# Doubled transfers and an fe row layout by transposing DMA in a joint-network training step

## The chip, the core and the metric

The kernel runs on one core of a Trainium2 chip. The metric is the device time of one execution in microseconds (us). The times below are of several executions; one more execution was recorded by the hardware profiler, and every profile line here comes from such a recording.

## The reference, cut to what matters

The reference computes a small speech model forward and then all gradients. Two convolutions of three taps with stride 2 and a tanh-approximated gelu turn `x` (2 x 16000 x 256) into `f` (2 x 4000 x 256). The joint network adds a projection of `f` to one of `g` (8 rows a batch), takes a tanh and projects again.

```python
h = gelu(conv3(x, w1))[:, ::2, :]
f = gelu(conv3(h, w2))[:, ::2, :]
fe = einsum("btd,de->bte", f, w_f)
ge = einsum("bud,de->bue", g, w_g)
j  = tanh(fe[:, :, None, :] + ge[:, None, :, :])
out = einsum("btud,dv->btuv", j, w_o)
# and the gradients of x, w1, w2, g, w_f, w_g, w_o for a given grad_out (2, 4000, 8, 256)
```

All inputs and outputs are bf16.

## The kernel before

The 4000 rows of `f` in each batch are cut into chunks: 256, seven of 512 and 160 rows in the first batch, seven of 512, then 256 and 160 in the second, 18 in all. A chunk whose rows are a multiple of 128 is called whole; the two of 160 rows aren't. In a whole chunk partition p holds nb adjacent rows (nb = 2 or 4), so that block a of 128 columns holds rows nb*p + a.

The main loop (L1170) runs over steps. Step k holds three stages of three different chunks side by side:

- `stage_j` of chunk k, the joint network. It runs over four pairs of `u` (`pair`, L759). For a pair, ACT makes `JT` = tanh(fe + ge) in column layout (channels on partitions, L766), while DVE adds (`JR`, L779) and ACT takes the tanh (L786) of the same values in row layout (rows on partitions), from `FER`, the row-layout fe. PE makes the output from `JT` and `WO`, the gradient of `w_o` from `JR` and the rows of grad_out (`GO_R`), and the gradient of `j` from the transposed grad_out (`GOT`). DVE multiplies the latter by 1 - j^2 (`JSQ`, `NGZ`) and sums over `u` in `ZS`. The output leaves through `OUT_SB`.
- `stage_a` of chunk k+1: the odd and even columns of the first convolution (`HTo`, `HTe`), the second convolution (`FT`), and `FE`, each with the gelu's derivative (`G1o`, `G1e`, `G2`). `shift` (L357) makes the column shifted by one row across blocks in a tile of its own: `HS` of `HTo`, `G1S` of `G1o`. `to_rows` (L642) turns `FE` into `FER` by TensorE transposes and one copy from PSUM.
- `stage_de` of chunk k-1: the backward pass through both convolutions and all weight gradients but that of `w_o`. The row layouts it needs (`HRo`, `HRs`, `HRe`, `FR`, `NFR`, `GFR`, `GHoR`, `GHeR`) are made by transposing DMAs within SBUF (`dma_rows`, L621). The gradient of `x` leaves through `GX_SB`, one block of 128 rows at a time.

All loads and all transposing DMAs are issued by SP, one instruction stream in order; all stores of outputs by POOL. Matmuls stand in one helper line, L412. `psb` is a PSUM tile of bf16, `ps` one of fp32.

The order of instructions on each engine is fixed by a planner in the kernel itself (`Flow`, L44 to L263). Every operation has a cost estimate, a due time and the buffers it needs. The planner simulates the engines, orders the operations by due time, then goes back from the end three times to set new due times, and keeps the best order. A DMA is taken to be done its queue's work plus 2.0 us plus a margin after its issue; the margin is 6.5 us (`MARGIN`, L49) unless the operation says otherwise. Each class of buffers is a ring with a fixed number of slots (L336); an operation that opens a new buffer waits in the plan until a slot is free.

Of the kernel before, what the change touches and what calls it, by code (L numbers as in the profile page):

```python
# [10 lines left out]
BF16 = mybir.dt.bfloat16  # L11
FP32 = mybir.dt.float32
ALU = mybir.AluOpType
# [265 lines left out]
def kernel(  # L279
# [56 lines left out]
    for name, n in (("xc", 1), ("xh", 2), ("xs", 1), ("hto", 2), ("hs", 2), ("ft", 2), ("g1e", 3), ("g1o", 3), ("g1s", 3), ("g2", 3),  # L336
                    ("fe", 2), ("fer", 2), ("gsq", 2), ("gs", 2), ("jt", 3), ("got", 3), ("go", 7), ("out", 6), ("rows", 4),
                    ("hte", 2), ("jr", 3), ("hro", 2), ("hrs", 2), ("hre", 2), ("fr", 2), ("jsq", 2), ("ngz", 2), ("ghe", 1), ("gho", 1),
                    ("ghs", 1), ("gf", 1), ("gfs", 1), ("gfh", 2), ("ngfe", 1), ("x5", 2), ("gx", 3), ("ghh", 2)):
        F.cls(name, n)  # L340
# [145 lines left out]
    def load_got(g_, up, h, at):  # L486
        S = st[g_]
        if h == 0:
            S.setdefault("GOT", {})[up] = buf("got", [P, NB, 2, KT, P], BF16, "GOT")
        GOT, GO = S["GOT"][up], S["GO"][up, h]  # L490
        dma("SP", lambda: GOT[:, 2 * h:2 * h + 2].rearrange("p a u k q -> p (a u k) q"),
            lambda: GO[:].rearrange("p a u v -> p (a u v)"), r=[GO], w=[(GOT, h)], bytes_=2 * P * 1024,
            new=[GOT] if h == 0 else [], transpose=True, at=at, margin=2000.0 if g_ == 0 else None)

    def load_gor(g_, up, h, at, hold=()):
        b, ci, c0, W = chunks[g_]
        GO = buf("go", [P, 2, 2, V], BF16, "GO_R")
        lo, hi = 2 * h * P, min(W, (2 * h + 2) * P)
        nb, rem = (hi - lo) // P, (hi - lo) % P
        src = grad_out[b, c0 + lo:c0 + hi, 2 * up:2 * up + 2, :].rearrange("t u v -> t (u v)")  # L500
        if whole[g_]:
            rows_ = grad_out[b, c0:c0 + W, 2 * up:2 * up + 2, :].rearrange("(p a) u v -> p a (u v)", p=P)
            dma(LOADQ, lambda: GO[:].rearrange("p a u v -> p a (u v)"), lambda: rows_[:, 2 * h:2 * h + 2], r=[], w=[(GO, "m")],
                bytes_=2 * P * 1024, new=[GO], at=at, hold=hold, margin=2000.0 if g_ == 0 else None)
            nb = rem = 0
# [8 lines left out]
        st[g_].setdefault("GO", {})[up, h] = GO  # L514
# [65 lines left out]

    def conv_gelu(W, taps, h_buf, h_ap, g_buf, g_ap, news):

        sq = buf("gsq", [P, KT, CW], BF16, "g_sq")
        s = buf("gs", [P, KT, CW], BF16, "g_s")
        for mt in range(KT):
            ps = psum()

            def mms(e, mt=mt, ps=ps):
# [9 lines left out]
                out=h_ap(mt), in_=ps[:, :W], func=ACT.Gelu_apprx_tanh), r=[ps], w=[(h_buf, mt)])  # L598
# [12 lines left out]
            out=sq[:, :, :W], in0=sq[:, :, :W], in1=h_ap(None), op=ALU.mult), r=[sq, (h_buf, 0), (h_buf, 1)], w=[sq], at=late)  # L611
# [51 lines left out]
    def stage_a(g_, t0, dt):  # L663
# [3 lines left out]
        HTo = colbuf("hto", g_, "HTo")  # L667
        G1o = colbuf("g1o", g_, "G1o")
        HTe = colbuf("hte", g_, "HTe")
        G1e = colbuf("g1e", g_, "G1e")  # L670
        S["HTo"], S["G1o"], S["G1e"] = HTo, G1o, G1e
        both = lambda T_: (lambda mt: T_[:, mt, 0:W] if mt is not None else T_[:, :, 0:W])
# [3 lines left out]
        conv_gelu(W, (taps, S["XCk"] + [W1]), HTo, both(HTo), G1o, lambda: G1o[:, :, 0:W], [HTo, G1o])  # L676
        shifted = []
        for cls, nm, T_ in (("hs", "HTo", HTo), ("g1s", "G1o", G1o)):
            if ci == 0:
                h, hr = None, []  # L680
            else:
                pv, pw = st[g_ - 1][nm], chunks[g_ - 1][3]
                h, hr = (lambda pv=pv, pw=pw: pv[:, :, pw - 1:pw]), [(pv, 0), (pv, 1)]
            shifted.append(shift(cls, g_, cls.upper(), lambda lo, hi, T_=T_: T_[:, :, lo:hi], [(T_, 0), (T_, 1)], h, hr))
        HS, S["G1S"] = shifted
# [4 lines left out]
        conv_gelu(W, (taps, S["XCk"] + [W1, S["XS"]]), HTe, both(HTe), G1e, lambda: G1e[:, :, 0:W], [HTe, G1e])  # L690
        pad_tail(g_, HTo)
        pad_tail(g_, HTe)
# [4 lines left out]
        taps = [(lambda i=i, kt=kt: W2[:, i, kt], 0, lambda SRC=SRC, kt=kt: SRC[:, kt, 0:W])  # L697
                for i, SRC in ((2, HTo), (1, HTe)) for kt in range(KT)]
        taps += [(lambda kt=kt: W2[:, 0, kt], lo, lambda f=f, kt=kt: f(kt)) for lo, f in back(g_, HS, HTo, W) for kt in range(KT)]
        S["go"] = [conv_gelu(W, (taps, [(HTo, 0), (HTo, 1), HS, (HTe, 0), (HTe, 1), W2]), FT, both(FT), G2,  # L700
                             lambda: G2[:, :, 0:W], [FT, G2])]
# [3 lines left out]
        S["FE"] = FE  # L705
        for mt in range(KT):
            ps = psum()

            def mms(e, mt=mt, ps=ps):
                for kt in range(KT):  # L710
                    mm(ps[:, :W], WF[:, kt, mt * P:(mt + 1) * P], FT[:, kt, :W], kt == 0, kt == KT - 1)
            pe_first(mt == 0, "fe", c_pe([W] * KT), mms, r=[(FT, 0), (FT, 1), WF], w=[ps], new=[ps] + ([FE] if mt == 0 else []))
            evac(lambda mt=mt: FE[:, mt, :W], lambda ps=ps: ps[:, :W], W, r=[ps], w=[(FE, mt)])
        pad_tail(g_, FE)
        S["FER"] = to_rows("fer", FE, 0, nb_of[g_] * P, [0, 1, "z"])
        F.now = t0 + A_AT[3] * dt
        late = [start_of[g_] + HR_AT[2] * W] * 2 if g_ < 2 else [t0 + HR_AT[0] * dt, t0 + HR_AT[1] * dt]
        HRo = col_rows("HRo", "hro", g_, HTo, ["z"], late[0])
        R0 = dma_rows("HRs", "hrs", g_, lambda: HS[:].rearrange("p k w -> p (k w)"), [HS], 1, late[0])
        if wh:  # L720
            S["HRs"] = [R0, HRo], lambda m, bl, d2: HRo.cols(m, bl - 1, d2) if bl else R0.cols(m, 0, d2)
        else:
            R1 = buf("hrs", [P, KT * P], BF16, "HRs")
            for kt in range(KT):
                dma("SP", lambda kt=kt: R1[:, kt * P:(kt + 1) * P], lambda kt=kt: HTo[:, kt, P - 1:2 * P - 1],
                    r=[(HTo, kt), (HTo, "z")], w=[(R1, kt)], bytes_=P * P * 2, new=[R1] if kt == 0 else [], transpose=True, nb=late[0])
            S["HRs"] = [R0, R1], lambda m, bl, d2: R1[:m, d2 * P:(d2 + 1) * P] if bl else R0.cols(m, 0, d2)
        HRe = col_rows("HRe", "hre", g_, HTe, ["z"], late[1])
        FR = col_rows("FR", "fr", g_, FT, ["z"], late[0])
        for nm, R in (("HRo", HRo), ("HRe", HRe), ("FR", FR)):  # L730
            S[nm] = [R], R.cols
# [24 lines left out]
    def stage_j(g_, t0, dt):  # L756
        b, ci, c0, W = chunks[g_]
        S = st[g_]
        def pair(up):  # L759
# [4 lines left out]
            for j in range(2):  # L764
                for mt in range(KT):
                    op("ACT", c_act(W, ptr=True), lambda e, j=j, mt=mt: nc.scalar.activation(  # L766
                        out=JT[:, j, mt, :W], in_=S["FE"][:, mt, :W], func=ACT.Tanh,
# [6 lines left out]
            for h, tbs in enumerate(halves):  # L774
# [15 lines left out]
                GO = S["GO"].pop((up, h))  # L790

                def gwo(e, tbs=tbs, JR=JR, GO=GO):
                    for tb, m in tbs:
                        for j in range(2):
                            for d2 in range(KT):
                                n = gwo_cnt[0]
                                mm(GWO[:, d2, :], JR[:m, tb % 2, j, d2 * P:(d2 + 1) * P], GO[:m, tb % 2, j, :],
# [3 lines left out]
            OUTS = [buf("out", [P, 2, 2, V], BF16, "OUT_SB") for _ in halves]  # L801
            for step in range(4):
# [41 lines left out]
                for tb, m in nblk[g_]:  # L844
# [3 lines left out]
                    OUT = OUTS[tb // 2]  # L848

                    def out_mm(e, tb=tb, m=m, ps=ps):  # L850
                        for jj in range(2):
# [3 lines left out]
                    pe_first(tb % 2 == 0, "out", c_pe([V] * 4), out_mm, r=[JT, WO], w=[ps], new=[ps] + ([OUT] if tb % 2 == 0 else []))  # L855
                    evac(lambda tb=tb, m=m, OUT=OUT: OUT[:m, tb % 2].rearrange("p u v -> p (u v)"), lambda m=m, ps=ps: ps[:m, :], 512,
                         r=[ps], w=[(OUT, tb % 2)])
            for h, OUT in enumerate(OUTS):
                F.now = tu + q * (h + 1) / 2
                lo, hi = 2 * h * P, min(W, (2 * h + 2) * P)  # L860
                nb, rem = (hi - lo) // P, (hi - lo) % P
                dst_ = out_0[b, c0 + lo:c0 + hi, 2 * up:2 * up + 2, :].rearrange("t u v -> t (u v)")
                if whole[g_]:
                    rows_ = out_0[b, c0:c0 + W, 2 * up:2 * up + 2, :].rearrange("(p a) u v -> p a (u v)", p=P)
                    dma(STOREQ, lambda rows_=rows_, h=h: rows_[:, 2 * h:2 * h + 2],
                        lambda OUT=OUT: OUT[:].rearrange("p a u v -> p a (u v)"), r=[OUT], w=[], bytes_=2 * P * 1024)
                    continue
                if nb:
                    dma(STOREQ, lambda dst_=dst_, nb=nb: dst_[0:nb * P].rearrange("(a p) n -> p a n", p=P),
                        lambda OUT=OUT, nb=nb: OUT[:, 0:nb].rearrange("p a u v -> p a (u v)"),  # L870
                        r=[(OUT, t_) for t_ in range(nb)], w=[], bytes_=nb * P * 1024)
                if rem:
                    dma(STOREQ, lambda dst_=dst_, nb=nb: dst_[nb * P:],
                        lambda OUT=OUT, nb=nb, rem=rem: OUT[:rem, nb].rearrange("p u v -> p (u v)"),
                        r=[(OUT, nb)], w=[], bytes_=rem * 1024)
# [351 lines left out]
```

## Time and profile before

| | us |
|---|---|
| median of 8 runs | 802.78 |
| lowest and highest run | 801.51, 805.07 |
| profiled execution, device time | 801.51 |
| its span, first to last instruction | 799.7 |
| mean granted TensorE clock | 0.997 of full speed |

The profiled execution is the lowest of the eight runs. PE is TensorE's matmuls, PEld its weight loads, DVE the vector engine, ACT the scalar engine, POOL GpSimd, SP the engine that issues DMAs. Busy shares are of the span; a pipelined matmul is recorded for longer than the time until the next one ends, so PE's share isn't its share of peak. The DMA share is the mean over 16 DMA engines of the time that packets took; packets overlap, so it can exceed 1. A waiting time is idle time of an engine just before an instruction, with what ended it.

The DMA queue of SP moved 133.25 MB, that of POOL 49.19 MB; all together 184.74 MB, 231 GB/s on average.

### The profile page before, as it was taken

How to read it: one execution, taken by the hardware profiler on the slowest of the kernel's cores; microseconds unless marked ns; L12 is line 12 of the kernel's file. 1: busy time of each engine (PE TensorE's matmuls, PEld its weight loads, DVE VectorE, ACT ScalarE, POOL GpSimd, SP SyncE). 2: the span in 40 equal slices, each digit the busy share in tenths (PEclk: the TensorE clock that was granted, in tenths of full speed). 3: DMA queues.
4: the chain of work that ended last, by engine and by line, in shares of the span. 5: the costliest groups of instructions: out<-in, count | busy, mean ns of one | idle time of the engine just before them, and what ended most of it. 6: DMA issues, size and time to landing. Idle time of an engine off the chain costs nothing.

```text
span 799.7 us, 17623 instructions
## 1 busy us (share of the span) xinstructions
PE 776.3 (97%) x6196; PEld 576.7 (72%) x6196; DVE 753.8 (94%) x1756; ACT 715.0 (89%) x1164; POOL 221.5 (28%) x461
## 2 busy tenths in 40 slices
PE   8788999999999999999999999999999999999997
PEld 6555667686776867787776668676776767778885
DVE  5999999998989999997989999999999999999995
ACT  5999999999999999997899999989898999898572
POOL 1212232321222222343232142222223132233242
PEclk9999999999999999999999999999999999999999
DMA  8999999999999999999999999999999899999974
GB/s 202 229 207 217 212 248 259 248 224 259 201 266 216 257 259 233 238 247 255 222 224 228 220 211 244 225 254 259 254 239 263 199 216 259 250 236 235 206 203 114
DMA packets 384700, 184.74 MB, mean 231 GB/s; under 512 B 331716, under 2 KB 368358, under 8 KB 384612
## 3 DMA queue, kind: packets, MB, share of 16 engines
q1 hardware_dynamic: 366644, 133.25, 86.8%
q0 software_dynamic: 15584, 49.19, 19.2%
q10 hardware_dynamic: 2384, 1.18, 0.6%
q8 instruction: 48, 0.79, 0.5%
q14 instruction: 40, 0.33, 0.1%
HBM read 52.48 MB, written 50.34 MB: 129 GB/s over the span
## 4 chain that ended last, share of the span: by engine, by line
PE 72%; DVE 11%; ACT 3%; DMA 1%; issue 1%; DVEq 0%; ACTq 0%
PE ps L412 61%; PE GWO L412 10%; DVE NGZ L833 2%; DVE ZS L841 2%; DMA GFR<-GF 1%; DVE JR L779 1%; DVE g_s L599 1%; DVE GHo L954 1%; DVE ACC L894 1%; PE psb L652 1%; DVE GHe L964 1%; ACT JR L786 1%; DVE g_sq L610 0%; DVE G1o L617 0%; DVE g_sq L607 0%
## 5 line engine op out<-in xcount | busy, mean ns | idle before, releaser
L766 ACT ACTIVATE JT<-FE,GE 128x512 bf16<-128x512 bf16 (+2 forms) x288 | 181.9, 676 | 5.7 <-PE ps L412 5.7
L440 POOL DMA_DIRECT2D out_dram<-OUT_SB x136 | 95.0, 700 | 243.4 <-ACT OUT_SB L423 151.7
L412 PE MATMUL ps<-GOT,WT 128*128 128x512 bf16 (+3 forms) x640 | 151.8, 334 | 2.7 <-DMA GOT<-GO_R 2.0
L412 PE MATMUL ps<-WO,JT 128*128 128x256 bf16 x1024 | 151.8, 273 | 2.3 <-DVE NGZ L833 0.8
L833 DVE SCALAR_TENSOR_TENSOR NGZ<-JSQ,ps 128x512 f32<-128x512 bf16 (+2 forms) x252 | 151.0, 605 | 2.0 <-PE ps L412 1.8
L786 ACT ACTIVATE JR<-JR 128x1024 bf16<-128x1024 bf16 x128 | 136.3, 1069 | 6.2 <-DVE JR L779 6.1
L412 PE MATMUL GWO<-GO_R,JR 128*128 128x256 bf16 x1024 | 132.4, 273 | 2.3 <-ACT JR L786 2.3
L823 ACT ACTIVATE JSQ<-JT 128x1024 bf16<-128x1024 bf16 (+2 forms) x132 | 126.5, 959 | 8.8 <-DVE NGZ L833 6.9
L412 PEld LDWEIGHTS <-JT 128*128 128x128 bf16 x1024 | 98.6, 98 | 47.3 <-issue 5.7
L841 DVE TENSOR_TENSOR ZS<-ZS,NGZ 128x512 f32<-128x512 f32 (+2 forms) x216 | 130.9, 613 | 0.1
L423 ACT CAST OUT_SB<-ps 128x512 bf16<-128x512 f32 x208 | 119.0, 597 | 8.5 <-PE ps L412 8.3
L412 PEld LDWEIGHTS <-JR 128*128 128x128 bf16 x1028 | 99.7, 98 | 25.4 <-ACT JR L786 3.4
L412 PEld LDWEIGHTS <-WT 128*128 128x128 bf16 x1000 | 88.4, 98 | 39.0 <-issue 3.8
L412 PEld LDWEIGHTS <-W 128*128 128x128 bf16 x792 | 69.6, 98 | 55.2 <-issue 2.9
L412 PE MATMUL ps<-XC,W 128*128 128x512 bf16 (+4 forms) x432 | 92.6, 342 | 2.2 <-DMA XC<-in_x_dram 1.2
L779 DVE TENSOR_TENSOR JR<-FER,GEB 128x1024 bf16<-128x1024 bf16 x128 | 87.3, 684 | 0.1
L412 PEld LDWEIGHTS <-X 128*128 128x128 bf16 x768 | 74.9, 98 | 10.7 <-issue 0.2
L440 POOL DMA_DIRECT2D out_dram<-GX_SB x70 | 38.9, 557 | 145.7 <-ACT GX_SB L425 113.5
L599 DVE SCALAR_TENSOR_TENSOR g_s<-g_sq,ps 128x512 bf16<-128x512 bf16 (+2 forms) x108 | 65.7, 609 | 9.9 <-ACT HTo L597 8.2
L412 PE MATMUL ps<-WT,GHo 128*128 128x256 bf16 x384 | 73.0, 273 | 0.2
L894 DVE TENSOR_TENSOR ACC<-ACC,ps 128x512 f32<-128x512 f32 x96 | 64.2, 676 | 9.3 <-PE ps L412 9.1
L595 ACT ACTIVATE g_sq<-ps 128x512 bf16<-128x512 f32 (+2 forms) x108 | 58.4, 546 | 9.3 <-PE ps L412 8.9
(137 smaller groups left out, 1280.8 us busy)
## 6 DMA issues: line engine op xcount, KB each, us to landing
GO_R<-in_grad_out_dram SPq DMA_DIRECT2D x120, 256.0 KB, 4.2
out_dram<-OUT_SB POOLq DMA_DIRECT2D x120, 256.0 KB, 4.7
X<-in_x_dram SPq DMA_DIRECT2D x28, 576.0 KB, 6.3
out_dram<-GX_SB POOLq DMA_DIRECT2D x60, 256.0 KB, 4.5
GOT<-GO_R SPq DMA_TRANSPOSE x128, 5.3
out_dram<-w_out SPq DMA_DIRECT2D x9, 128.0 KB, 2.0
GO_R<-in_grad_out_dram SPq DMA_DIRECT2D x8, 128.0 KB, 3.7
out_dram<-OUT_SB POOLq DMA_DIRECT2D x8, 128.0 KB, 3.2
```

Of the source, the lines that this page charges most:

```text
L412: nc.tensor.matmul(ps_ap, lhsT=lhsT, rhs=rhs, start=start, stop=stop)
L423: nc.scalar.copy(out=dst(), in_=src())
L440: return eng_.dma_start(out=out(), in_=in_())
L595: op("ACT", c_act(W, True), lambda e, mt=mt, ps=ps: nc.scalar.activation(out=sq[:, mt, :W], in_=ps[:, :W], func=ACT.Square, scale=GELU_SQR ...
L599: op("DVE", c_dve(W), lambda e, mt=mt, ps=ps: nc.vector.scalar_tensor_tensor(out=s[:, mt, :W], in0=sq[:, mt, :W], scalar=1.0, in1=ps[:, :W ...
L766: op("ACT", c_act(W, ptr=True), lambda e, j=j, mt=mt: nc.scalar.activation(out=JT[:, j, mt, :W], in_=S["FE"][:, mt, :W], func=ACT.Tanh, bi ...
L779: op("DVE", c_dve(n * 2 * D, 0.5), lambda e, lo=lo, n=n, m=m, JR=JR: nc.vector.tensor_tensor(out=JR[:m, lo % 2:lo % 2 + n], in0=S["FER"][: ...
L786: op("ACT", c_act(n * 2 * D), lambda e, lo=lo, n=n, m=m, JR=JR: nc.scalar.activation(out=JR[:m, lo % 2:lo % 2 + n], in_=JR[:m, lo % 2:lo % ...
L823: nc.scalar.activation(out=JSQ[:, :, :W], in_=JT[:, j, :, :W], func=ACT.Square)
L833: op("DVE", c_dve(W) + 6, lambda e, d2=d2, ps=ps, u=u, zap=zap, JSQ=JSQ: nc.vector.scalar_tensor_tensor(out=zap(), in0=JSQ[:, d2, :W], sca ...
L841: op("DVE", c_dve(W), lambda e, d2=d2, dst=dst, NGZ=NGZ: nc.vector.tensor_tensor(out=dst[:, d2, :W], in0=ZS[:, d2, :W], in1=NGZ[:, :W], op ...
L894: op("DVE", c_dve(512), lambda e: nc.vector.tensor_tensor(out=acc_ap().rearrange("p k d -> p (k d)"), in0=acc_ap().rearrange("p k d -> p ( ...
```

## The change

In words:

- `GO_R`, `GOT` and `OUT_SB` hold all blocks of a chunk for a pair of `u` and are moved by one DMA instead of one for each half. Rings: `go` 7 halves to 4 wholes, `out` 6 halves to 3 wholes.
- In whole chunks, two blocks of `GX_SB` share one tile and leave with one DMA, with 4 KB instead of 2 KB in a row. Ring `gx` 3 single to 2 double.
- In whole chunks `FE` lies block-major (block, then half of the channels), written and read through strided patterns, and `FER` is made by one transposing DMA on SP. The 160-row chunks keep the TensorE transposes.
- `HTo` and `HTe` lie in one tile `HT`, the shifted block in front of `HTo`; one DMA makes `HR` out of all three. `G1o` has its shifted block in front too. The second convolution then reads each tap of `HTo` in one run, and `GHo` takes one DVE instruction instead of two. Rings: `hto`, `hte`, `hs` of 2 become `hh` of 2; `hro`, `hrs`, `hre`, `fr` of 2 become `hr`, `hrs`, `fr` of 1.
- `GHo` and `GHe` lie in one tile `GH`, and one DMA makes `GHR`. Ring `rows` 4 to 2, `ghr` 1.

```diff
-    ... ("hto", 2), ("hs", 2), ("ft", 2), ("g1e", 3), ("g1o", 3), ("g1s", 3), ("g2", 3),
-        ("fe", 2), ("fer", 2), ("gsq", 2), ("gs", 2), ("jt", 3), ("got", 3), ("go", 7), ("out", 6), ("rows", 4),
-        ("hte", 2), ("jr", 3), ("hro", 2), ("hrs", 2), ("hre", 2), ("fr", 2), ("jsq", 2), ("ngz", 2), ("ghe", 1), ("gho", 1),
-        ("ghs", 1), ("gf", 1), ("gfs", 1), ("gfh", 2), ("ngfe", 1), ("x5", 2), ("gx", 3), ("ghh", 2)):
+    ... ("hh", 2), ("ft", 2), ("g1e", 3), ("g1o", 3), ("g2", 3),
+        ("fe", 2), ("fer", 2), ("gsq", 2), ("gs", 2), ("jt", 3), ("got", 3), ("go", 4), ("out", 3), ("rows", 2), ("ghr", 1),
+        ("jr", 3), ("hr", 1), ("hrs", 1), ("fr", 1), ("jsq", 2), ("ngz", 2), ("gh", 1),
+        ("ghs", 1), ("gf", 1), ("gfs", 1), ("gfh", 2), ("ngfe", 1), ("x5", 2), ("gx", 2), ("ghh", 2)):
...
+    def load_got(g_, up, at):
+        S, n = st[g_], nb_of[g_]
+        GOT, GO = buf("got", [P, NB, 2, KT, P], BF16, "GOT"), S["GO"][up]
+        S.setdefault("GOT", {})[up] = GOT
+        dma("SP", lambda: GOT[:, 0:n].rearrange("p a u k q -> p (a u k) q"),
+            lambda: GO[:, 0:n].rearrange("p a u v -> p (a u v)"), r=[GO], w=[GOT], bytes_=n * P * 1024,
+            new=[GOT], transpose=True, at=at, margin=2000.0 if g_ == 0 else None)
...
+    def part(B_, view):
+        p_ = Buf(None, None, None, B_.name)
+        p_.view = lambda _: view(B_.t)
+        return p_
...
+        HT = buf("hh", [P, KT * (2 * CW + P)], BF16, "HT")
+        HTo = part(HT, lambda t_: t_[:, 0:ns].rearrange("p (k w) -> p k w", k=KT))
+        HTe = part(HT, lambda t_: t_[:, ns:ns + nc_].rearrange("p (k w) -> p k w", k=KT))
...
-                for i, SRC in ((2, HTo), (1, HTe)) for kt in range(KT)]
-        taps += [(lambda kt=kt: W2[:, 0, kt], lo, lambda f=f, kt=kt: f(kt)) for lo, f in back(g_, HS, HTo, W) for kt in range(KT)]
+                for i, SRC, lo in ((2, HTo, P), (1, HTe, 0), (0, HTo, r0)) for kt in range(KT)]
...
+        if wh:
+            FE.view = lambda t_: t_[:, 0:KT * n * P].rearrange("p (b k q) -> p k b q", k=KT, q=P)
...
-        S["FER"] = to_rows("fer", FE, 0, nb_of[g_] * P, [0, 1, "z"])
+        if wh:
+            FR_ = S["FER"] = buf("fer", [P, NB, D], BF16, "FER")
+            dma("SP", lambda: FR_[:, 0:n].rearrange("p b (k q) -> p (b k) q", q=P), lambda: FE.t[:, 0:KT * n * P],
+                r=[(FE, 0), (FE, 1)], w=[FR_], bytes_=KT * n * P * P * 2, new=[FR_], transpose=True)
+        else:
+            pad_tail(g_, FE)
+            S["FER"] = to_rows("fer", FE, 0, n * P, [0, 1, "z"])
...
-        HRo = col_rows("HRo", "hro", g_, HTo, ["z"], late[0])
-        R0 = dma_rows("HRs", "hrs", g_, lambda: HS[:].rearrange("p k w -> p (k w)"), [HS], 1, late[0])
...
-        HRe = col_rows("HRe", "hre", g_, HTe, ["z"], late[1])
-        FR = col_rows("FR", "fr", g_, FT, ["z"], late[0])
+        HR = buf("hr", [P, KT * (2 * CW + P)], BF16, "HR")
+        dma("SP", lambda: HR.t[:, 0:ns + nc_].rearrange("p (g q) -> p g q", q=P), lambda: HT.t[:, 0:ns + nc_], r=[HT], w=[HR],
+            bytes_=(ns + nc_) * P * 2, new=[HR], transpose=True, nb=late[0])
...
+        FR = col_rows("FR", "fr", g_, FT, ["z"], late[1])
...
-            OUTS = [buf("out", [P, 2, 2, V], BF16, "OUT_SB") for _ in halves]
+            OUT = buf("out", [P, NB, 2, V], BF16, "OUT_SB")
...
+        GHR = buf("ghr", [P, 2 * KT * CW], BF16, "GHR")
+        dma("SP", lambda: GHR.t[:, 0:2 * nc_].rearrange("p (g q) -> p g q", q=P), lambda: GH.t[:, 0:2 * nc_], r=ghk, w=[GHR],
+            bytes_=2 * nc_ * P * 2, new=[GHR], transpose=True)
...
+                    dma(STOREQ, lambda s0=s0 - 1, sn=sn, lo=lo, hi=hi, dst=dst: bass.AP(
+                        tensor=dst.tensor, offset=dst.offset + (4 * (s0 + sn * lo) - 3) * D, ap=[[4 * sn * D, hi - lo], [1, 8 * D]]),
+                        lambda GX2=GX2, lo=lo, hi=hi: GX2[:].rearrange("p a c d -> p (a c d)")[lo:hi], r=[GX2], w=[],
+                        bytes_=(hi - lo) * 4096, cost=550.0)
```

`GO_R`'s load, which now fetches a whole pair, has the same form as the new `load_got`. `late` holds the earliest due times of the row layouts: 0.7 (`late[0]`) and 0.4 (`late[1]`) of the step before the chunk's own.

## The prediction

> **What bounds the kernel now.** I read the page's busy shares first, then the busy time by stages, then the chain of waits inside one step, then the groups by form, the waits and the DMA issues.
>
> ```profile
> PE 776.3 (97%) x6196; PEld 576.7 (72%) x6196; DVE 753.8 (94%) x1756; ACT 715.0 (89%) x1164; POOL 221.5 (28%) x461
> ```
>
> Three engines are near full, so the page's shares don't say which one sets the end. Time by stages (columns: stretch, length, then busy us and instruction count of PE, PEld, DVE, ACT, POOL, then PE clock, DMA share, GB/s):
>
> ```profile
> 0.00:80.00 80.00, 67.20 (x515) 47.34 (x516) 69.22 (x183) 69.99 (x123) 16.67 (x44) 0.98 1.01 214
> 80.00:360.00 280.00, 278.25 (x2154) 203.87 (x2154) 271.56 (x594) 266.37 (x417) 76.94 (x154) 1.00 1.12 240
> 360.00:480.00 120.00, 117.82 (x951) 85.89 (x950) 112.26 (x269) 108.20 (x180) 36.39 (x76) 1.00 1.10 227
> 480.00:760.00 280.00, 278.66 (x2225) 210.64 (x2223) 270.34 (x613) 249.71 (x402) 76.04 (x154) 1.00 1.10 238
> 760.00:800.00 40.00, 34.35 (x359) 28.98 (x357) 30.40 (x101) 20.68 (x45) 15.48 (x35) 0.98 0.62 158
> ```
>
> From 80 to 760 us PE idles 5.3 of 680 us. PE's idle time lies at the ends: 12.8 us in the first 80 (there DVE and ACT are the full ones) and 5.7 in the last 40. Is a busy PE really at its rate? The chain, one whole 512-row step (start us, us, what):
>
> ```profile
> 234.34 4.76 PE ps L412 x26
> ...
> 259.55 0.87 PE GWO L412 x8
> 260.42 0.45 PE psb L652 x8
> 260.87 2.39 PE ps L412 x18
> ...
> 281.79 4.76 PE ps L412 x26
> ```
>
> Every piece between is PE; the same work starts again after 47.45 us. Eight 256-column matmuls take 0.87 us (109 ns each), two 512-column ones 0.43 (217 ns each), so 0.417 ns a column plus some 2.8 ns a matmul. A whole step's code holds 111,616 moving columns in 364 matmuls (49,152 in the joint stage, 18,432 in the convolutions, 2,048 and 1,024 for fe and its transposes, 40,960 in the backward stage): 46.5 + 1.0 = 47.5 us, what the chain shows. So in the long middle PE is the bound with no hidden slack, and its removed columns come off one for one. The eight fe transposes of a step stand in that chain with 0.45 us (56 ns each).
>
> **What the Trainium skill says.** "Perfetto Trace Analysis", section "Identifying the Most-Contended Engine": matmul busy share is no good measure because matmuls are pipelined. Agreed, hence the column count: a group mean says 219 ns a transpose, the chain 56. "TensorE: Matmul & The Clock Gate", "Part 4: PE-mode transpose": the result lands in PSUM, so a copy must follow, and one cost about 275 ns in a kernel. The copy is there (below); here back-to-back ones cost a fifth of that. "VectorE: DVE Perf Modes", "The three transpose paths": 1309 ns for a 128x128 block by DMA against 390 by TensorE; a latency, which decides only where nothing covers it. "DMA: Bandwidth & Descriptors", "Latency and other measured facts": 261 GB/s for transposing DMAs with a non-contiguous middle dimension. No stretch here holds transposes alone, so I use this only for an estimate.
>
> **The change part by part.** The groups concerned, by form (busy us, mean ns, idle before):
>
> ```profile
> L412 PE MATMUL ps<-HS,W 128*128 128x128 bf16 x72 | 9.9, 219 | 0.0
> L423 ACT COPY FER<-psb 128x1024 bf16<-128x1024 bf16 x8 | 8.1, 1014 | 0.0
> L428 DVE COPY FER<-psb 128x1024 bf16<-128x1024 bf16 x6 | 4.1, 676 | 0.0
> L954 DVE SCALAR_TENSOR_TENSOR GHo<-G1o,ps 128x384 bf16<-128x384 bf16 x28 | 15.2, 543 | 0.0
> L954 DVE SCALAR_TENSOR_TENSOR GHo<-G1S,ps 128x128 bf16<-128x128 bf16 x36 | 9.9, 276 | 0.4 <-PE ps L412 0.4
> ```
>
> 1. *fe by DMA in the 16 whole chunks.* PE loses 14 x 8 + 2 x 4 = 120 transposes x 56 ns = 6.7 us. The two 160-row chunks keep theirs. ACT loses 8 x 1.01 + some 0.6 = 8.7 us, DVE 6 x 0.68 + 0.4 = 4.5. Added: 16 transposing DMAs, 3.9 MB.
> 2. *One conv2 tap run instead of two (HS, HTo).* Columns stay, 4 matmuls a chunk go: 72 x 2.8 ns = 0.2 us of PE.
> 3. *GHo in one DVE instruction.* The 512-column form of its neighbour GHe takes 676 ns, the pair 543 + 276 = 819: 0.143 x 28 = 4.0 us of DVE, some 0.5 more in the small chunks.
> 4. *Block-strided fe in the evacuation and the tanh.* Same elements in runs of 128. Bounded by nothing and by one short instruction's overhead per run; 160-column forms, strided already, cost no more per element than the 256-column ones (G1e: 317 for 320, 408 for 512). I take nothing.
> 5. *Doubled GO_R, GOT, OUT and GX, merged HR and GHR.* Bytes stay nearly the same. SP is an in-order queue. The smallest issue times are 1.17 us for a 64 KB HRs, 1.23 for a 256 KB GOT, 1.45 for a 512 KB XC: mostly per instruction. Before: 308 transposes, about 385 us of SP. After: 72 GOT, 32 XC, 18 HR, 54 FR, NFR and GFR, 18 GHR, 16 FER and 4 R1, 214 in all, about 290. SP and POOL (136 OUT stores at 0.70 us become 72 whole, 8 of them small remainders aside) get slack, which no one waits for today.
> 6. *Buffers.* GO_R goes from 7 halves to 4 pairs, OUT from 6 halves to 3 pairs, GX from 3 single blocks to 2 doubles: the same room or more. HR and FR go from two buffers to one. HR(k) can now load only after the weight gradients of chunk k-1 in step k, about a third into it, and is read a third into step k+1: some 45 us for a landing of 6. HT has two buffers and holds until then. Hidden; without that cover each chunk would show about 6 us.
>
> ```profile
> GOT<-GO_R SPq DMA_TRANSPOSE x128, 5.3
> ...
> HRe<-HTe SPq DMA_TRANSPOSE x18, 3.8
> ...
> GFR<-GF SPq DMA_TRANSPOSE x18, 5.2
> ```
>
> 7. *DMA load.* 184.7 MB become 188.6; over 795 us 237 GB/s. Stretches of 280 to 315 GB/s occur today (315 from 35 to 40 us), so the engines aren't at their limit. At the skill's 261 GB/s, FER costs 15 us of DMA time in all, an estimate, hidden under PE.
> 8. *The wait added.* JR's add on DVE waits for FER. Behind it in DVE's order stand the Z updates and gelu terms, and PE waits for those. In the middle fe is ready by 260.4 us and its next step's first JR falls due half a pair, about 6 us, ahead of 281.8, so 15 us cover 1.3 us of issue and a landing near 5; the planner itself reckons 2 + 6.5 us plus work. Uncovered is the start: fe of chunk 0 is written by 20.3 us, FER was ready at 22.0 and JR ran at 22.4. By DMA it is ready at 26 at the earliest and planned near 30, with SP still on the first GOTs. GO_R's four buffers are then freed later, so chunk 1's first pair loads later. I bound this from -1 us (DVE and ACT, full there, lose about 2 us of work between them) to +6 (the whole delay shows as PE idle) and take +1: other work is at hand, and PE waits there for GOT anyway:
>
> ```profile
> PE ps L412 <- DMA GOT<-GO_R: 2.0, 1, 2.0
> ```
>
> The sum: -6.7 - 0.2, of which some 0.8 falls where PE doesn't bind, leaves -6.1; the start +1; in the middle 5.3 us of stalls, some on DVE and ACT, shrink with 8.7 and 9.0 us less work there: -1. Together -6. The profiled execution took 801.5 us (span 799.7 and 1.8 around it), so 795.5. It was the fastest of the runs, whose median is 1.3 higher: 796.5.
>
> **The rivals.**
> *A, the sum above.* PE stays the bound. 790 to 800.
> *B, no change.* The transposes go, but stalls of 0.3 to 0.5 us a chunk, in the start or before JR, hand it back: 801.2 to 804.4. For it: DVE is at 97% and ACT at 95% in the middle, so any order made worse shows. Against: both lose work.
> *C, slower.* The queue's own granularity. A 512 KB GOT, or a 0.59 MB HR (18 blocks), stands ahead of GFR, NFR, FER and GHR on SP's one queue. These are on the way between two PE stages; they land in about 5 us today, GFR up to 9.3, and the planner allows some 9 to 10. One more 256 KB in front is about 1.0 us by the 261 GB/s estimate; two, with the single-buffered HR issued close to them, 2. GFR once stood in the chain with 8.2 us and PE idled 0.4 at that place, so the allowance is already touched. It decides from 0.33 us of new PE stall a chunk (6.0/18), when the gain is gone. At 1 us a chunk the time is 796.5 + 18 = 814.5, at 2 us 832.5. For it: DMA share above 1 in the middle. Against: fewer instructions, no queueing by issue, and PE waited for a GOT just once.
> That the change fails to do what it says is excluded for the transposes, which its branch replaces; that the transfers' size matters at all is what the profile doesn't support.
>
> **How the numbers follow.** A 56%, B 10%, C 34%; C gets that much because the plan of all engines is rebuilt and three of them stand within 6% of full. Predicted 796.5. A's own range is 789 to 801. With C's lower half taken in, 789 to 813 leaves out a few per cent below and some 15 above. About 0.2%, 1.6 us, is what a measurement of this kernel tells from no change: faster 0.57, same 0.09, slower 0.34.
>
> **What would show it.** Right: PE transposes 8 (plus the weights'), step time in the middle 47.0 instead of 47.45, no PE wait on FER, SP waiting more than now. Wrong: PE idle in the middle above 12 us with DMA or JR behind it (C), or a start past 80 us with more than 18 us of PE idle (B, from step 8).

## The result, and the profile after

| | before | after |
|---|---|---|
| median, us | 803.10 (33 runs) | 811.31 (12 runs) |
| lowest and highest run | 800.92, 806.12 | 806.01, 821.93 |
| ratio, 95% interval | 1 | 1.0096 [1.0077, 1.0116] |
| profiled execution, us | 801.51 | 811.71 |

The change made the kernel about 1% slower; the forecast was 796.5 us. The changed kernels scatter far more from run to run than the kernel before, and the ratios leave out runs over 1.5% above the fastest of their kernel (two of the twelve here) while the medians take all, so the ratios are read first and a difference of two or three microseconds between two changed kernels carries little.

The busy shares of the changed kernel:

```profile
PE 773.9 (96%) x6004; PEld 566.9 (70%) x6004; DVE 748.8 (92%) x1713; ACT 708.5 (87%) x1154; POOL 162.7 (20%) x376
```

All three full engines are busy for less time than before, and the span is 10.1 us longer: time went into idleness. Busy time by stages (columns as in the prediction) says where:

```profile
0.00:80.00 80.00, 67.08 (x491) 46.42 (x492) 66.99 (x177) 68.25 (x121) 14.84 (x41) 0.96 1.03 218
80.00:360.00 280.00, 269.94 (x2028) 194.32 (x2027) 262.03 (x558) 259.56 (x409) 51.61 (x120) 1.00 1.08 238
360.00:480.00 120.00, 114.91 (x909) 82.96 (x908) 108.73 (x262) 102.47 (x170) 25.85 (x59) 1.00 1.10 231
480.00:760.00 280.00, 277.84 (x2142) 205.88 (x2140) 271.19 (x593) 253.93 (x405) 54.32 (x121) 1.00 1.09 243
```

The start is as it was (12.9 us of PE idle in the first 80, 12.8 before). The first half of the middle isn't: PE idles 10.1 us from 80 to 360 us where it idled 1.8, and 5.1 where it idled 2.2 in the next stretch. From 80 to 760 that makes 17.3 us instead of 5.3. The waits of the changed kernel (us in total, times, longest):

```profile
PE ps L412 <- DMA GOT<-GO_R: 7.0, 4, 2.1
...
DVE JR L811 <- DMA FER<-FE: 6.1, 2, 3.5
```

PE now waits for `GOT` four times, DVE twice for the new `FER`. PE's own waits for `GOT` are 7.0 of the 17.3 us; no single line holds the rest. The chain of before ran through PE for 72% of its length; now it does for 39%. Long pieces of it (start us, us, what) are:

```profile
128.91 7.94 DMA FER<-FE
...
180.20 10.21 DMA GOT<-GO_R
...
226.85 13.15 DMA GOT<-GO_R
...
278.38 10.58 DMA GOT<-GO_R
```

These `GOT`s take 10 to 13 us from issue to landing; the median of the page is 7.2. The timeline around the longest, SP first:

```profile
221.11 2.92 SPq L438 DMA_TRANSPOSE HR<-HT  x1
224.13 1.26 SPq L438 DMA_TRANSPOSE FER<-FE  x1
225.49 1.27 SPq L440 DMA_DIRECT2D GO_R<-in_grad_out_dram  x1
226.85 5.33 SPq L438 DMA_TRANSPOSE GOT<-GO_R  x1
```

and POOL in the same stretch (in brackets the idle time before, and what ended it):

```profile
225.75 0.55 POOL L440 DMA_DIRECT2D out_dram<-GX_SB  x1 [10.49 <-ACT GX_SB L425]
227.66 0.71 POOL L440 DMA_DIRECT2D out_dram<-OUT_SB  x1 [1.35 <-ACT OUT_SB L423]
230.68 0.55 POOL L440 DMA_DIRECT2D out_dram<-GX_SB  x1 [2.31 <-ACT GX_SB L425]
```

SP puts `HR` (0.59 MB), `FER` and `GO_R` ahead of the `GOT`; in the same five microseconds POOL sends three stores of 512 KB each. The two late `GOT`s at 180 and 278 us have the same company: an `HR` and a `FER` on SP, a 512 KB `OUT_SB` and two 512 KB `GX_SB` on POOL. The Trainium skill ("DMA: Bandwidth & Descriptors", section "Queues, rings and completion order") says that each DMA engine takes turns between the queues that have work for it, so a store on POOL's queue takes its share of the engines that SP's transposes need. The lines agree with that in time and place, but no line shows the turns themselves; whether the store is the cause the experiments have to say.

### The profile page after: what moved, and what is told of

The parts are those of the page before. It is cut to its first block, busy times and chain, and to the rows that moved or that the text cites. A ratio compares the mean times of both kernels' runs of the same rounds, so it can differ in the third digit from the quotient of the medians.

```text
span 809.8 us, 16667 instructions
## 1 busy us (share of the span) xinstructions
PE 773.9 (96%) x6004; PEld 566.9 (70%) x6004; DVE 748.8 (92%) x1713; ACT 708.5 (87%) x1154; POOL 162.7 (20%) x376
## 4 chain that ended last, share of the span: by engine, by line
PE 39%; ACT 24%; DVE 23%; DMA 9%; issue 4%; DVEq 0%; SPq 0%; ACTq 0%
PE ps L412 33%; ACT JT L798 6%; PE GWO L412 6%; DMA GOT<-GO_R 5%; DVE NGZ L865 5%; ACT JR L818 4%; ACT JSQ L855 4%; DVE ZS L873 4%; ACT OUT_SB L423 3%; DVE g_s L603 2%; DMA FER<-FE 2%; DVE JR L811 2%; ACT g_sq L599 2%; DMA XC<-in_x_dram 2%; ACT g_s L609 1%
## 5 line engine op out<-in xcount | busy, mean ns | idle before, releaser
L855 ACT ACTIVATE JSQ<-JT 128x1024 bf16<-128x1024 bf16 (+2 forms) x133 | 128.6, 967 | 15.1 <-DVE NGZ L865 13.7
L423 ACT CAST OUT_SB<-ps 128x512 bf16<-128x512 f32 x202 | 117.1, 598 | 15.3 <-PE ps L412 15.1
L412 PEld LDWEIGHTS <-W 128*128 128x128 bf16 x720 | 66.4, 99 | 60.0 <-issue 6.7
L440 POOL DMA_DIRECT2D out_dram<-OUT_SB x80 | 54.6, 683 | 242.5 <-ACT OUT_SB L423 154.3
L412 PE MATMUL ps<-WT,GH 128*128 128x256 bf16 x732 | 98.0, 273 | 2.0 <-DVE g_s L603 0.7
L412 PE MATMUL ps<-GHR,X 128*128 128x256 bf16 x768 | 91.5, 273 | 0.2 <-DMA GHR<-GH 0.2
L412 PEld LDWEIGHTS <-GH 128*128 128x128 bf16 x732 | 71.2, 98 | 16.1 <-issue 2.3
L922 DVE TENSOR_TENSOR ACC<-ACC,ps 128x512 f32<-128x512 f32 x96 | 64.1, 677 | 10.7 <-PE ps L412 10.2
```

Source lines behind the costliest of these rows:

```text
L412: nc.tensor.matmul(ps_ap, lhsT=lhsT, rhs=rhs, start=start, stop=stop)
L423: nc.scalar.copy(out=dst(), in_=src())
L440: return eng_.dma_start(out=out(), in_=in_())
L855: nc.scalar.activation(out=JSQ[:, :, :W], in_=JT[:, j, :, :W], func=ACT.Square)
L922: op("DVE", c_dve(512), lambda e: nc.vector.tensor_tensor(out=acc_ap().rearrange("p k d -> p (k d)"), in0=acc_ap().rearrange("p k d -> p ( ...
```

## The experiments

| kernel | `GO_R`, `GOT` | `OUT_SB` stores | fe rows | median | ratio to before, 95% |
|---|---|---|---|---|---|
| after | 512 KB | 1 x 512 KB | DMA | 811.31 | 1.0096 [1.0077, 1.0116] |
| e1 | 512 | 1 x 512 | TensorE | 814.65 | 1.0145 [1.0114, 1.0176] |
| e4 | 256 | 2 x 256 | DMA | 798.95 | 0.9943 [0.9918, 0.9968] |
| e12 | 256 | 2 x 256 | TensorE | 800.90 | 0.9979 [0.9969, 0.9989] |
| e9 | 256 | 1 x 512 | DMA | 818.01 | 1.0161 [1.0133, 1.0189] |
| e6 | 512 | 2 x 256, two buffers | DMA | 806.65 | 0.9969 [0.9946, 0.9992] |
| e10 | 512 | 2 x 256, one buffer | DMA | 801.59 | 0.9958 [0.9932, 0.9984] |
| e13 | 512 | 2 x 256, both late | DMA | 805.74 | 1.0013 [0.9990, 1.0035] |
| e16 | 512 | 2 x 256, by partitions | DMA | 846.03 | 1.0491 [1.0434, 1.0547] |
| e15 | 512 | 4 x 128 | DMA | 796.31 | 0.9926 [0.9907, 0.9945] |
| e18 | 256 | 4 x 128 | DMA | 806.48 | 1.0043 [1.0026, 1.0059] |
| e14 | 512 | as e10, `GX_SB` 256 KB | DMA | 805.05 | 1.0024 [1.0006, 1.0042] |
| e2 | before, fe by DMA alone | 2 x 256 | DMA | 814.28 | 1.0134 [1.0092, 1.0175] |
| e11 | before | 1 x 512 | TensorE | 806.96 | 1.0073 [1.0044, 1.0102] |
| e17 | before | 4 x 128 | TensorE | 804.34 | 1.0023 [1.0013, 1.0032] |

### Is it the fe DMA, or the size of the transfers? (e1 to e4)

e1 puts the TensorE transposes and the plain `FE` back into the changed kernel:

```diff
-        if wh:
-            FR_ = S["FER"] = buf("fer", [P, NB, D], BF16, "FER")
-            dma("SP", ...)
-        else:
-            pad_tail(g_, FE)
-            S["FER"] = to_rows("fer", FE, 0, n * P, [0, 1, "z"])
+        pad_tail(g_, FE)
+        S["FER"] = to_rows("fer", FE, 0, n * P, [0, 1, "z"])
```

> The changed kernel with its fe rows by TensorE transposes again, everything else of the change kept. Load theory (the transposing DMAs of SP's queue were as full as PE before; the 3.9 MB for fe are what is too much): back to 800 to 804 us, PE's waits for GOT gone. Grain theory (pieces twice as large hold SP and land late; fe's DMA is harmless): the 120 transposes come back on PE on top of the loss, 813 to 818. Late-JR theory (the row-layout fe lands too late for the DVE add at the start of a chunk): 800 to 804 as well, but GOT waits stay.

814.65 us: without the fe DMA the changed kernel is slower still, by 3.3 us (4 by the ratios). So the fe DMA isn't what made it slow.

e2 does the opposite, the same `FE` and `FER` hunks alone in the kernel before; e3 leaves the kernel before its transposes and adds 16 transposing DMAs of `FE` that nothing reads:

```diff
+        if wh:
+            n = nb_of[g_]
+            XX = buf("rows", [P, KT * NB * P], BF16, "FEX")
+            dma("SP", lambda: XX[:, 0:KT * n * P].rearrange("p (g q) -> p g q", q=P), lambda: FE.t[:, 0:KT * n * P],
+                r=[(FE, 0), (FE, 1)], w=[XX], bytes_=KT * n * P * P * 2, new=[XX], transpose=True)
```

> The kernel before with only the block-major fe and its transposing DMA; all other transfers, buffers and merges as before. Load: 806 to 811 us. Grain: the 6 us of PE work come off, 795 to 798. Late JR: 806 or more, with DVE's JR add waiting for FER at several chunks.

> The kernel before, fe rows still by TensorE, plus one transposing DMA of fe in each whole chunk whose result nobody reads. Load: 806 to 812 us, since the load alone costs. Grain and late JR: 802 to 804, no change.

814.28 and 814.51 us (ratio 1.0164 [1.0121, 1.0206] for e3). In the kernel before, 3.9 MB of transposing DMAs more cost some 11 us (11 and 13 by the ratios), whether DVE waits for them or nobody does: PE's 6.7 us less don't show in e2. e3's buffers come out of the ring of `NFR` and its like, and its plan moves the DMAs of SP by up to 19 places, so part of its loss can be that. Stages of e2:

```profile
80.00:360.00 280.00, 273.17 (x2086) 199.91 (x2099) 269.16 (x595) 263.07 (x415) 73.64 (x149) 1.00 1.13 248
360.00:480.00 120.00, 116.19 (x913) 84.25 (x918) 110.83 (x271) 104.06 (x172) 31.84 (x67) 0.99 1.06 228
480.00:760.00 280.00, 274.77 (x2149) 205.90 (x2163) 266.70 (x607) 258.22 (x421) 75.80 (x150) 1.00 1.12 244
```

PE idles 15.9 us from 80 to 760 us (5.3 before) while the DMA engines move 248 GB/s in the first stretch, more than before. That isn't a ceiling that only e2 meets: e4 and e10, both faster than the kernel before, move 248 GB/s there too. The load costs time in this kernel; that the engines ran out isn't shown.

e4 keeps the fe DMA and all merged tiles of the change and puts `GO_R`, `GOT` and `OUT_SB` back to halves (rings 7, 3 and 6):

```diff
-            OUT = buf("out", [P, NB, 2, V], BF16, "OUT_SB")
+            OUTS = [buf("out", [P, 2, 2, V], BF16, "OUT_SB") for _ in halves]
...
-        GO = st[g_].setdefault("GO", {})[up] = buf("go", [P, NB, 2, V], BF16, "GO_R")
+        GO = buf("go", [P, 2, 2, V], BF16, "GO_R")
```

> The changed kernel with GO_R, GOT and OUT_SB in halves again (7, 3 and 6 buffers as before); fe's DMA, merged HR and GHR and doubled GX stay. Load: still 807 to 812 us. Grain: 795 to 799. Late JR: 807 to 812.

798.95 us: 12 us off the changed kernel, and faster than the kernel before. So what cost the time lies in these three transfers and their rings.

### Is it SP's queue, or the plan? (e5, e7, e8)

e5 leaves `GO_R` and `OUT_SB` whole and makes each `GOT` with two transposing DMAs of 256 KB:

```diff
+        for h in range((n + 1) // 2):
+            lo, hi = 2 * h, min(n, 2 * h + 2)
+            dma("SP", lambda lo=lo, hi=hi: GOT[:, lo:hi].rearrange("p a u k q -> p (a u k) q"), ..., w=[(GOT, h)], ...)
```

> The changed kernel with GOT made by two 256 KB transposing DMAs from the whole GO_R; GO_R, OUT_SB and all else whole. Grain by GOT (one 512 KB transpose holds SP some 3.9 us and everything behind it): 798 to 802 us. Grain by GO_R's or OUT_SB's whole tiles: still 808 to 813. Fullness of SP's stream by instructions (56 more of them): 812 or more.

826.06 us (1.0288 [1.0262, 1.0315]), and PE waits longer for the smaller pieces:

```profile
PE ps L412 <- DMA GOT<-GO_R: 21.3, 9, 5.7
```

So the size of a `GOT` isn't the trouble by itself. The number of SP's instructions isn't either: e4 has the same 128 `GOT`s and more loads and transposes on SP in all (456 against 400), and is fast. Why two halves behind one whole load are this slow stays open.

e7 is the kernel before with one constant of the planner changed (PE's wake-up cost 45 to 46), to see what another plan alone does. e8 is the changed kernel with the planner told what the trace shows, that a large transposing DMA holds SP longer:

```diff
-        c = 1260.0 if transpose else 400.0 if q == "SP" else ...
+        c = 1260.0 + max(0.0, bytes_ - 262144.0) / 262144.0 * 2000.0 if transpose else 400.0 if q == "SP" else ...
```

> The kernel before with one constant of its planner moved from 45 to 46 ns (the wake-up time of PE), which reorders some instructions and changes nothing else. If any new plan costs some per cent by chance, this shows it: 800 to 806 us says that plan noise is below 0.4%; 808 or more says that the size of the effects in the other runs can't be put down to their edits alone.

> The changed kernel with one line of the planner changed: a transposing DMA above 256 KB is planned to hold SP for 1.26 us plus 2 us for each further 256 KB instead of 1.26 us flat. If the changed kernel loses because its plan doesn't know how long SP is held, the new order recovers most: 798 to 804 us. If the hold itself is the cost, whatever the order: 808 to 813.

802.65 (1.0000 [0.9983, 1.0018]) and 809.16 us (1.0100 [1.0052, 1.0148]). Another plan moves the kernel before by nothing, and better knowledge of SP doesn't mend the changed one. e7 reorders ACT and DVE, but leaves 468 of SP's 494 loads and transposes in their places; and a single perturbation doesn't bound what plans do to the changed kernel. That stays untested.

### Which of the three transfers? (e6, e9, e11)

e6 halves `OUT_SB` alone, e9 `GO_R` and `GOT` alone (each by its part of e4's diff); e11 makes `OUT_SB` whole in the kernel before.

> The changed kernel with OUT_SB alone in halves (6 buffers, a store for each half); GO_R and GOT whole. Grain by OUT_SB (evacuations wait for a whole tile's store): 798 to 802 us. Grain by GO_R or GOT: still 808 to 813.

> The changed kernel with GO_R and GOT in halves (7 buffers of 256 KB, one 256 KB load and one 256 KB transpose each) and OUT_SB left whole; with the run that halved OUT_SB alone (806.65) and the one that halved all three (798.95) it splits the 12 us that the larger transfers cost. Theory 1, the 512 KB store of OUT_SB is what makes the transposes of GOT late: most of the loss stays, 806 to 810 us, and PE still waits some 5 us on GOT in the stretch 80 to 360. Rival, the 512 KB load GO_R in front of a 512 KB GOT on SP's queue is: 799 to 802 us.

> The kernel before with OUT_SB alone whole (3 buffers of 512 KB, one 512 KB store). Theory 1, the large store costs by itself what halving it gave back in the changed kernel: 807 to 812 us. Rival, it costs only beside the 512 KB loads and transposes of the changed kernel: 802 to 804 us.

e6: four runs at 799.7, 801.4, 811.9 and 812.0; its ratio, 0.9969, rests on the two lower. e9: 818.01. e11: 806.96. With `OUT_SB` whole instead of in halves the time is 10 us longer by the ratios beside 512 KB loads (after against e6), 17 beside 256 KB ones (e9 against e4, 0.0218 of 803) and 6 in the kernel before (e11): the same sign three times, in kernels with different plans. Halving `GO_R` and `GOT` has no sign of its own: beside a whole `OUT_SB` it costs 5 us (e9 against after), beside half ones it gains 2 (e4 against e6), within the scatter.

### What about the store? (e10, e13, e16, e14)

e10 keeps the whole `OUT_SB` and its ring of 3, and stores it by two DMAs, the first as soon as two blocks are there:

```diff
-                dma(STOREQ, lambda: rows_, lambda: OUT[:, 0:nb_of[g_]]..., r=[OUT], w=[], bytes_=W * 1024)
+                for h in range(nb_of[g_] // 2):
+                    F.now = tu + q * (h + 1) / 2
+                    dma(STOREQ, lambda h=h: rows_[:, 2 * h:2 * h + 2], lambda h=h: OUT[:, 2 * h:2 * h + 2]...,
+                        r=[(OUT, 2 * h), (OUT, 2 * h + 1)], w=[], bytes_=2 * P * 1024)
```

> The changed kernel with OUT_SB a whole buffer as it is (3 of 512 KB), but stored by two DMAs of 256 KB, the first as soon as its two blocks are there. Theory 1, the size and moment of the store matter: as with OUT_SB in halves, 801 to 807 us. Rival, the buffer matters (a whole OUT_SB comes free later than two halves): 810 to 812 us, as the changed kernel, and ACT or DVE wait on OUT_SB's store.

801.59 us: this edit alone takes the loss back (ratio 1.0096 to 0.9958, 11 us). The buffers are the same, so it is the store, or the plan that comes with it. Its waits:

```profile
DVE JR L811 <- DMA FER<-FE: 1.9, 1, 1.9
...
PE ps L412 <- DMA GOT<-GO_R: 1.8, 1, 1.8
```

They were 6.1 and 7.0 us. It isn't that `GOT` lands sooner in general. From 80 to 760 us, the changed kernel's `GOT`s first, then those of e10:

```profile
DMA to landing us min/median/max: 3.3/7.9/13.2
...
DMA to landing us min/median/max: 3.3/7.3/13.6
```

The long ones fall elsewhere: the four `GOT`s for which PE waited in the changed kernel took 10.2, 13.2, 10.6 and 8.8 us; in e10 three of the same four took 7.3, 6.3 and 5.8 (the landing of the other isn't in the trace), and its three longest, 12.4 to 13.6 us, stand where PE needs them only 19 to 25 us after their issue.

Is it the plan? The edit touches nothing on SP, and the order of SP's 344 loads and transposes hardly changes: none moves by more than five places. But in the steps at 178, 224 and 276 us the changed kernel issues `HR` ahead of `FER`, and e10 `FER` ahead of `HR`, so e10 alone doesn't part the store from this order. Two kernels speak against the order as the cause: e8 has `HR` first in 2 of 13 steps (the changed kernel in 5, e10 in 3) and stays slow, and e1 has no `FER` DMA in its whole chunks and stays slow. The orders of DVE and ACT change far more in every one of these kernels; that part of the rival stands untested.

PE's idle time from 80 to 760 us falls from 17.3 to 9.8:

```profile
80.00:360.00 280.00, 276.16 (x2093) 202.45 (x2108) 271.20 (x579) 269.35 (x426) 71.01 (x148) 1.00 1.10 248
360.00:480.00 120.00, 118.03 (x925) 85.12 (x930) 114.86 (x270) 105.31 (x173) 33.38 (x71) 1.00 1.11 231
480.00:760.00 280.00, 276.03 (x2154) 208.01 (x2168) 267.71 (x602) 246.11 (x399) 69.15 (x138) 1.00 1.10 241
```

e13 has the same two stores, but both with `r=[OUT]`, after the last block. e16 also waits for the last block and splits by partitions:

```diff
+                for h in range(2):
+                    dma(STOREQ, lambda h=h: rows_[64 * h:64 * h + 64],
+                        lambda h=h: OUT[64 * h:64 * h + 64, 0:nb_of[g_]]..., r=[OUT], w=[], bytes_=W * 512)
```

> The changed kernel with OUT_SB whole and stored by two DMAs of 256 KB, both only when its last block is there. Theory 1, the moment decides (half of the store goes a half pair earlier, so that it doesn't meet the transposes in one burst): 809 to 813 us, as the changed kernel. Rival, what goes out in one DMA decides (its size, or its 4 KB rows): 799 to 804 us, as with the early split.

> The changed kernel with OUT_SB whole and stored by two DMAs of 256 KB, both when its last block is there, the first of partitions 0 to 63 and the second of 64 to 127, so that the rows stay 4 KB long. Theory 1 (the moment): 809 to 813 us. Rival, the size of one DMA: 799 to 804 us. Second rival, the length of the rows: 809 to 813 us here while the two late stores with 2 KB rows come to 799 to 804 us.

e13, 805.74 us, lies between: by the ratios the two late stores recover 0.0083 of the 0.0138 that the early ones do. Taken at its word, both count, the moment and what goes out in one DMA, and none of the expected answers held alone; its runs scatter from 798 to 816 us. The length of the rows isn't what the engines see: the packets of both stores are 4096 bytes in the trace, nearly as many in every kernel here (11,904 or 11,934).

e16 is 35 us slower than the changed kernel, with the same size in one DMA as e13:

```profile
PE ps L412 <- DMA GOT<-GO_R: 33.9, 12, 8.8
...
DVE JR L811 <- DMA FER<-FE: 22.4, 4, 11.1
```

The Trainium skill ("SBUF — State Buffer", section "Door 1: The DMA port swizzle (why `[64,N]` ≈ `[32,N]`)") says that partitions 0 to 63 reach only 8 of the 16 ports between DMAs and SBUF, measured there as 196 GB/s against 328 for all 128 with 1 MiB. The trace doesn't name ports; it agrees in that the 4096-byte packets of stores take 235 ns here and 197 in the changed kernel, though e4, whose stores span all 128 partitions, has 214. The stores land in 6.1 us (median of the 256 KB ones), the changed kernel's 512 KB ones in 5.9; of the transposes, `GOT` takes 7.7 us against 7.2 and `HR` 8.3 against 6.9. SP's order is close to the changed kernel's, no load or transpose more than two places off, though `HR` stands ahead of `FER` more often (8 of 12 steps). So a change to the stores on POOL's queue goes with later transposes on SP's; by what path isn't shown.

e14 adds to e10 the `GX_SB` buffers and stores of 256 KB of the kernel before (ring 4).

> The changed kernel with OUT_SB stored by two DMAs as its blocks come, and GX_SB in buffers and stores of 256 KB as in the kernel before (4 buffers instead of 2 of 512 KB). If a 512 KB store costs wherever it falls, as 56 stores of OUT_SB cost 10 us, the 28 of GX_SB cost some 5: 795 to 799 us, and the fastest version. Rival, GX_SB's stores meet nothing that PE waits for: 800 to 804 us, as with OUT_SB's two stores alone.

805.05 us, 3.5 more than e10 (5 by the ratios) and not less: the doubling of `GX_SB` isn't a cost, though its stores stand in the same bursts. A store of 512 KB isn't bad wherever it falls.

### Is smaller always better? (e15, e17, e18) And is the fe DMA worth it? (e12)

e15 is e10 with four stores of 128 KB, each after its block; e17 puts the same four stores into the kernel before, e18 into e4.

> The changed kernel with OUT_SB whole and stored by four DMAs of 128 KB with rows of 1 KB, each as soon as its block is there. If smaller and earlier stores go on to help: 796 to 800 us, below the 801.59 of two stores. If the loss was only that of one late 512 KB burst, nothing more comes: 801 to 804 us.

> The kernel before with each OUT_SB half stored by two DMAs of 128 KB, each as soon as its block is there, instead of one of 256 KB. Theory 1, small stores leave the loads and transposes their place on the DMA engines in any kernel: 796 to 800 us (half of what going from one store to four gave in the changed kernel was from 512 to 256 KB, which the kernel before has already, and the other 5 us are left). Rival, the kernel before isn't held up by its stores of 256 KB, and the gain needs what the change takes off PE: 802 to 804 us.

> The changed kernel with GO_R and GOT in halves and OUT_SB in halves, each half stored by two DMAs of 128 KB. If the size of GO_R and GOT costs by itself: 790 to 795 us, the fastest. If it doesn't, and only the store's size did: 795 to 799 us, as with the four stores beside the whole GO_R and GOT (796.31) or the halves with two stores (798.95).

e15 is the fastest kernel of this study, 796.31 us, 0.74% under the kernel before. Its PE idles 7.3 us from 80 to 760:

```profile
80.00:360.00 280.00, 276.97 (x2098) 202.70 (x2114) 272.86 (x588) 267.33 (x425) 86.72 (x191) 1.00 1.12 246
360.00:480.00 120.00, 117.36 (x921) 85.19 (x926) 112.67 (x265) 104.92 (x173) 39.77 (x86) 1.00 1.09 237
480.00:760.00 280.00, 278.39 (x2194) 210.98 (x2208) 272.73 (x617) 245.56 (x404) 85.30 (x188) 1.00 1.11 244
```

But e17 is 804.34 and e18 806.48: in the kernel before the small stores gain nothing (2 us slower by the ratio), in e4 they cost 8 us. That is nearly as much as the whole store costs, from an edit that was expected to help, and whether it is the stores or the plan isn't known. No rule in the size of a store or a load alone gives all these times. What holds without exception is that each of the six kernels with the whole late store (after, e1, e5, e8, e9, e11) is slower than the kernel before.

e12 is e4 with e1's edit.

> The changed kernel with GO_R, GOT and OUT_SB in halves and, besides, fe's rows by TensorE transposes and the plain FE: what is left of the change are the merged HT, HR, GH, GHR and the 512 KB GX_SB. Theory 1, the fe DMA pays for itself wherever it isn't late (the 3 us of the run without it in the changed kernel, up to the 6 us of PE work): 802 to 805 us. Rival, FER's 4 MB are what the DMA engines lack, as 11 us in the kernel before with the fe DMA alone suggest: 788 to 795 us.

800.90 us. By the ratios the fe DMA gains 3 us beside halves, 4 beside whole transfers (e1), and loses 11 in the kernel before. What lies between the kernel before and e12 are the merged tiles. From 80 to 760 us, fewer than eight packets were in flight during 26 us of the kernel before, 39 of e12 and 11 of e4, as if the merged tiles left room on the DMA engines that `FER` fills. But e1, in which there was no more room than before (24 us), gains from `FER` as well, and the changed kernel then stands at 24 too. So why `FER` pays in two kernels and costs in the third isn't shown.

## Why the prediction was wrong

**Step 1, the transposes and copies off PE, ACT and DVE: right in the work, too large in the time.** Between e12 and e4 PE's busy time falls by 5.3 us (773.4 to 768.1; I said 6.7), and the time by 2 to 3. The rest becomes idle time: from 80 to 760 us PE idles 7.9 us in e12 and 11.9 in e4. "One for one" did not hold.

**Steps 2 to 4: right in what can be read.** `GHo` is one instruction of 676 ns, 28 times, as worked out. `FE`'s evacuation on ACT takes 589 ns instead of 581 and `JT`'s tanh 740 instead of 736: the block-strided patterns cost next to nothing. One reading behind step 4 was wrong all the same: 317 ns for 320 and 408 for 512 are 0.99 and 0.80 ns an element, so the smaller form did cost more for each; a fixed part of every instruction would explain that, and the answer came out right without it. And the figures of the chain, 109 and 217 ns, give 0.422 ns a column and 1.0 a matmul rather than 0.417 and 2.8; the 47.45 us of a step come out either way, and step 2's 0.2 us would be 0.1.

**Step 5 failed: the doubled `OUT_SB` store was put at nothing.** It came under "bytes stay nearly the same", with slack for SP and POOL "which no one waits for today". POOL's cheaper issue was looked at where the store itself should have been: one 512 KB store at the end of a pair, on the same DMA engines as `GOT` and `FER`. e10, which edits only that store, is 11 us faster, and in three other pairs of kernels the whole store costs 10, 17 and 6 us (after and e6, e9 and e4, e11 and before). As far as edits can show it, this is the term that turned the sign.

Step 5 was also wrong in "mostly per instruction", which took the smallest issue times for the usual ones. `GOT` took SP 1.85 us on average already before and takes 3.90 now, so 72 of them hold it 281 us where 128 held it 236; all transposes together 647 us where it was 604 (I said 290 from 385). But this isn't what cost the time: in e10 the 72 `GOT`s hold SP for 281 us as well.

**Step 7 failed in "hidden", not in the average.** The average was there: e15 moves the bytes of the changed kernel, 188.8 MB, in 796.31 us, and from 80 to 360 us e4 and e10 move 248 GB/s and e15 246, where the changed kernel moves 238. The row of DMA shares doesn't tell them apart; the changed kernel's, then that of e15:

```profile
DMA  8999999999999999899999999999999999999985
...
DMA  8999999999999999999999999999999999999986
```

Before, too, 36 of the 40 slices were at 9 or more. Neither this row nor a single slice of 280 to 315 GB/s says whether a transfer lands in time, and that was not asked of the larger loads and stores. The 3.9 MB of `FER` show how much hangs on what else is under way: they cost some 11 us in the kernel before (e2, e3) and nothing between e12 and e4.

**Step 8: the start was right, the middle not.** PE's idle time in the first 80 us didn't change (+1 taken, 0.1 found). In the middle the "15 us" of cover gave out twice, by 6.1 us in all, when `FER` (7.9 and 7.6 us from its issue until DVE went on) was issued behind an `HR` and a `GOT`. **Step 6 was right:** in the changed kernel PE and DVE never wait for the single `HR` or `FR`; POOL waits three times for `HR` to be read out of `HT`, 5.0 us in all.

**The rivals.** C had the direction, and part of the place: it named `FER` and `HR`, and all four long pieces shown above stand behind an `HR` on SP. But its cause, a long `GOT` in front of the transfers on SP's one queue, isn't what the runs show: a late one is `GOT` itself, halving `GO_R` and `GOT` doesn't help beside a whole store (e9), splitting `GOT` hurts (e5), and what takes the loss back is a store on another queue. PE's 17.3 us of idle time in the middle with DMA and `JR` behind it is the sign that I had named for C.

**What stays open.** Why one whole store costs 6 to 17 us when the bytes are the same, by what path, and how much is its moment and how much its size, isn't settled beyond e13's middle value. Why four stores help with 512 KB loads and hurt with 256 KB ones isn't either. Each edit also gives a new plan of DVE and ACT, and no run holds that fixed. That e15 ends at the predicted time (796.3) is luck and doesn't make the sum right; two of its terms were wrong.

## What to carry to other kernels

A row of DMA shares at nine tenths doesn't say whether more will fit: here it reads the same in the slowed kernel and in the fastest. Price each transfer by when it has to land and by what else is sent then, stores on another queue included. Before doubling a transfer, ask when its bytes go out: in this kernel a store that left in parts as its blocks came was better than one that left whole at the end, though dividing further helped in one kernel only. Try the merged pieces of a change one by one: here dividing one store again turned a loss of 1% into a gain of 0.4%. And where every edit makes a new plan, compare the orders of the queues before giving the edit all the credit.

## What the runs showed of the hardware

SP's time on a transposing DMA isn't a property of its size. At the very start the three `XC` loads of 512 KB, with nothing to wait for, held SP for 1.44, 4.04 and 5.31 us, 10.9 in all:

```profile
0.74 10.90 SPq L438 DMA_TRANSPOSE XC<-in_x_dram  x3
```

The bytes are the same each time; what differs is what was already under way. In the loop, too, a `GOT` of 256 KB holds SP for 1.66 us on average in e12 and 1.90 in e4, which adds `FER`. So the smallest issue time of a transposing DMA is no price for the rest. And a store split by partitions isn't a smaller store: e16, with half the bytes in each DMA, is 35 us slower than the changed kernel.
